# A first block that shares its engines with attention: router columns moved to another bank, loads and steps put in another order

## The chip, the cores and the metric

One core of one Trainium2 chip runs the kernel. The metric is the device time of one execution in microseconds. The median of three runs of the kernel before is 877.84 us (876.73 to 879.01). The engines go by these names: PE is TensorE (PEld its weight loads), DVE is VectorE, ACT is ScalarE, POOL is GpSimd, SP is SyncE, which here issues the DMA transfers in the order in which they are written.

## The reference

Three stages follow each other. The inputs of the attention are 32-bit floats; the weights of the first network come as 64-bit floats.

```python
# attention with a decaying state; B, H, S, D = 4, 8, 768, 48
for t in range(S):
    state = alpha[:, :, t, :, None] * state + einsum('bhd,bhe->bhde', k[:, :, t], v[:, :, t])
    y[:, :, t] = einsum('bhd,bhde->bhe', q[:, :, t], state)
x = y.transpose(0, 2, 1, 3).reshape(3072, 384)
# first network: w_in 384 x 2048, w_out 2048 x 384
h = x @ w_in
x = (h - tanh(h)) @ w_out
# second network: 8 experts, one for each token, w1[e] 384 x 1024, w2[e] 1024 x 384
logits = x @ w_gate;  e = argmax(logits);  p = softmax(logits)[e]
out = p * sigmoid((x @ w_output_gate)[e]) * (relu(x @ w1[e]) @ w2[e])
```

## The kernel before

The 3072 tokens are handled in eight blocks of 384 (`NBLK`, `TB`). For each block, attention has four units (`NP`, a pair of heads each), so unit `u` belongs to block `u // 4`. A unit is worked off in chunks of 64 tokens: `prep_k` (lines 169 to 176) makes the decayed keys `kh`, `prep_q1` and `prep_q2` the products of decays, their reciprocals and the scaled queries `X0`, `scale_k` the keys `kt` divided by the decays, `turn_k` the transposed keys `ktok`. `score` and `causal` give the masked scores, `carry`, `update` and `chain` the states, `readout` the outputs in two PSUM banks (`pair`), and `place` splits them into a rounded part and a rest and stores both with four or six DMAs into `xT`, the input of the first network (lines 307 to 324).

The first network has sixteen steps `f` for each block. `h_step` (lines 402 to 416) multiplies `xT` by the weights' columns (nine matmuls of 384 columns: high times high, high times low, low times high, for three parts of the inner dimension), takes the tanh on ACT, subtracts on DVE, rounds the high half of `gg` on ACT and takes the low half on DVE. `x_step` (lines 418 to 426) multiplies `gg` of the step before by the second weights into three accumulators `px[j][0]` to `px[j][2]`, one PSUM bank each, with nine matmuls of 400 columns: 384 of the output and 16 router columns, which are the second weights already multiplied by `w_gate` and `w_output_gate`.

The weights `WH` and `WL` stay on chip for all blocks; they are made while block 0 runs. For each step `load_w` brings 768 KB of 64-bit floats; `conv` narrows them with three integer instructions on DVE (`narrow`, lines 332 to 337) and issues the load for three steps later; `split_w` rounds the high part on ACT and takes the rest on POOL. `gate_turn` transposes the second weights on PE into the one bank `at` of `psa` and copies them to `wT`; `gate` multiplies `wT` by the router weights into 16 spare columns of an accumulator's bank and copies the high part on ACT; `gate_low` takes the rest on DVE.

Attention of unit 4 to 8 runs within the sixteen steps of block 0, in four phases `ph = f % 4`: scores and states in 0, the mask in 1, the readout in 2, turning and scaling keys in 3. In this block (`first_block`, lines 757 to 807, with the prologue above it) the order of PE, ACT, DVE, POOL and SP is the written one. From block 1 on a planner orders all engines but SP, and from block 2 on SP too. Before block 0 a prologue handles units 0 to 3. `bank` hands out the accumulators' banks in the prologue, and then the bank `at`. A tile's new contents wait until the last reader of the old contents in the same buffer has ended; a PSUM bank is watched as a whole.

Of the kernel before, what the change touches and what calls it, by code (L numbers as in the profile page):

```python
# [63 lines left out]
def tile_kernel(ctx, tc, aps, outs):  # L64
# [16 lines left out]
    ap2 = att.enter_context(tc.tile_pool(name="ap2", bufs=2, side="right"))  # L81
    rw = att.enter_context(tc.tile_pool(name="rw", bufs=2, side="right"))
    stg = att.enter_context(tc.tile_pool(name="stg", bufs=STG, side="right"))
    stg3 = att.enter_context(tc.tile_pool(name="stg3", bufs=2, side="right"))
    psx = mlp.enter_context(tc.tile_pool(name="psx", bufs=1, space=PSUM))
    psh = mlp.enter_context(tc.tile_pool(name="psh", bufs=2, space=PSUM))
    pss = ExitStack()
# [81 lines left out]
    def prep_k(u):  # L169
        s = st[u]  # L170
        a = s["raw"][:, 2 * TB:2 * TB + AW]
        Ex = ap1.tile([128, AW], F32, tag="Ex", name="Ex")
        s["kh"] = ap2.tile([128, NC, CH], F32, tag="kh", name="kh")
        yield dve.tensor_tensor_scan(out=Ex[:, ::-1], data0=a[:, ::-1], data1=ones1[:, ::-1],
                                     initial=0.0, op0=ALU.mult, op1=ALU.add)
        yield dve.tensor_tensor(out=s["kh"], in0=c3(s["raw"][:, 0:TB]), in1=c3(Ex[:, 1:AW])[:, :, 1:CH + 1], op=ALU.mult)
# [40 lines left out]

    def turn_k(u):
        s = st[u]
        ps = bank("pst")  # L220
        for i in range(NA):
            pe.transpose(ps[:, i * 128:(i + 1) * 128], s["kh"].rearrange("p c t -> p (c t)")[:, i * 128:(i + 1) * 128], ident)  # L222
        s["ktok"] = ap1.tile([128, NA, 128], F32, tag="ktok", name="ktok")
        act.copy(s["ktok"].rearrange("p a d -> p (a d)"), ps[:, 0:NA * 128])
# [140 lines left out]
    def gate_turn(f):  # L365
        ps = psa.tile([128, 512], F32, tag="at", name="pso")
        w = gw.pop(f)
        for k in range(KC):
            pe.transpose(ps[:, k * 128:(k + 1) * 128], w[:, DM + k * 128:DM + (k + 1) * 128], ident)
        gated[f] = wT = g3.tile([128, KC, 128], F32, tag="gg", name="wT")  # L370
        act.copy(wT.rearrange("p k c -> p (k c)"), ps[:, 0:DM])

    def gate(f):

        wT = gated.pop(f)
        pl = px[0][f % NA][:, DG + f // NA * 2 * E:DG + (f // NA + 1) * 2 * E]
        for k in range(KC):
            pe.matmul(pl, wT[:, k], wg[:, k], start=(f < 2 and k == 0), stop=(k == KC - 1), skip_group_check=True)
        c = slice(2 * DM, 2 * DM + 2 * E)
        act.copy(WH[:, f, c], pl)  # L380
        gated[f] = pl, c

    def gate_low(f):
        pl, c = gated.pop(f)
        dve.tensor_tensor(out=WL[:, f, c], in0=pl, in1=WH[:, f, c].bitcast(F32), op=ALU.subtract)  # L385

    def conv_next():
        nonlocal nconv
        nconv += 1
        return conv(nconv - 1)  # L390
# [25 lines left out]
        return gg  # L416

    def x_step(j, f, gg):
        if f == 0 and j:
            px[j] = [psx.tile([128, 512], F32, tag=f"x{a}", name=f"x{a}") for a in range(NA)]  # L420
        for a in range(NA):
            n = 0
            for gi, w in ((0, WH), (1, WH), (0, WL)):
                pe.matmul(px[j][a][:, 0:DG], gg[:, gi, a * 128:(a + 1) * 128], w[:, f, DM:],  # L424
                          start=(f == 0 and n == 0), stop=(f == NF - 1 and n == 2))
                n += 1
# [312 lines left out]
    K(NP)  # L739
    fill(4)  # L740
    weave(*half)
    split_w(1)
    gate_turn(0)
    h_begin(0, 0, range(KC - 1))
    weave(prep_q(NP))
    fill(12)
    h_begin(0, 1, range(KC - 1))
    alpha_low(NP)
    load_w_v(NP)
    load_w_v(NP + 1)  # L750
# [1 line left out]
    load_unit(NP + 2)  # L752
    dve.tensor_copy(trib, cst[:, 192:320])
    dve.tensor_copy(base, cst[:, 368:376])
    px[0] = [psx.tile([128, 512], F32, tag=f"x{a}", name=f"x{a}") for a in range(NA)]

    def first_block(f, pend):
        u, ph = NP + (f + 1) // 4, f % 4
        if ph == 0:
            carry(u)  # L760
        elif ph == 1:
            weave(causal(u))
        elif ph == 2:
            weave(prep_k(u + 1))
        else:
            weave(prep_q1(u))
        new = [conv_next()] if nconv < NF else []

        def head():

            gate(f)
            if ph == 0:
                score(u)
                update(u)
                load_v(u + 2)
            elif ph == 2:
                readout(u)
                load_unit(u + 3)
                load_w_v(u + 2)
            elif ph == 3:  # L780
                turn_k(u)
            for g in new:
                next(g, 0)
                next(g, 0)

        def middle():
            weave(*new)
            if ph == 0:
                weave(chain(u))
            elif ph == 3:  # L790
                scale_k(u)
                weave(prep_q2(u))

        gg = h_step(0, f, (head, middle))
        gate_low(f)
        if ph == 2:
            place(u)
        if pend:
            x_step(*pend)
        if new:  # L800
            split_w(f + 2)
        if f + 1 < NF:
            gate_turn(f + 1)
        if ph == 3:
            decay(u)
            alpha_low(u)
        return gg

    pend = None
# [381 lines left out]
```

## Time and profile before

| what | value |
|---|---|
| median of three runs | 877.84 us |
| the profiled execution | 873.37 us |
| its span, first to last instruction | 871.2 us |
| PE busy | 817.5 us, 94% |
| PE weight loads busy | 768.2 us, 88% |
| DVE busy | 473.2 us, 54% |
| ACT busy | 353.8 us, 41% |
| POOL busy | 160.9 us, 18% |

The prologue reaches to about 42 us, block 0 from there to 167, blocks 1 to 7 to 620, and the experts come after. Busy times are of one execution; idle time of an engine that nothing waits for costs nothing. In rows of a timeline the last column in brackets is the idle time ahead of the instruction and what ended it.

### The profile page before, as it was taken

How to read it: one execution, taken by the hardware profiler on the slowest of the kernel's cores; microseconds unless marked ns; L12 is line 12 of the kernel's file. 1: busy time of each engine (PE TensorE's matmuls, PEld its weight loads, DVE VectorE, ACT ScalarE, POOL GpSimd, SP SyncE). 2: the span in 40 equal slices, each digit the busy share in tenths (PEclk: the TensorE clock that was granted, in tenths of full speed). 3: DMA queues.
4: the chain of work that ended last, by engine and by line, in shares of the span. 5: the costliest groups of instructions: out<-in, count | busy, mean ns of one | idle time of the engine just before them, and what ended most of it. 6: DMA issues, size and time to landing. Idle time of an engine off the chain costs nothing.

```text
span 871.2 us, 16990 instructions
## 1 busy us (share of the span) xinstructions
PE 817.5 (94%) x6736; PEld 768.2 (88%) x6736; DVE 473.2 (54%) x1002; ACT 353.8 (41%) x767; POOL 160.9 (18%) x136
## 2 busy tenths in 40 slices
PE   6787867899999999999999999999999999999995
PEld 4576757799999999999899999999999999999995
DVE  7785876656655556565565563355543433434421
ACT  5444533533444434344343343235443434435431
POOL 0122312002010010010020020011233234324321
PEclk9778987999999999999999999999999999999998
DMA  9545343375323223223232320104264154245400
GB/s 273 172 155 164 105 132 90 120 239 167 97 84 98 68 82 97 65 87 93 67 89 65 94 63 22 28 29 145 95 218 154 65 188 169 87 154 199 150 25 28
DMA packets 64358, 98.54 MB, mean 113 GB/s; under 512 B 20235, under 2 KB 52768, under 8 KB 64272
## 3 DMA queue, kind: packets, MB, share of 16 engines
q1 hardware_dynamic: 60864, 87.91, 32.7%
q0 software_dynamic: 3408, 9.47, 2.9%
q8 instruction: 55, 0.90, 0.4%
q14 instruction: 31, 0.25, 0.1%
HBM read 72.13 MB, written 16.25 MB: 101 GB/s over the span
## 4 chain that ended last, share of the span: by engine, by line
PE 72%; issue 5%; DMA 3%; DVE 2%; ACT 1%; SPq 1%; POOL 1%; POOLq 0%; DVEq 0%; ACTq 0%
PE x L424 22%; PE psh L400 20%; PE o L949 10%; PE psf L921 10%; PE psy L302 3%; PE psy L238 2%; PE psu L264 2%; PE pst L900 1%; DMA wst<-wio 1%; PE pst L222 1%; DMA xT<-y 1%; DMA s<-w 1%; POOL out L967 1%; DMA raw<-raw 1%; SPq L321 0%
## 5 line engine op out<-in xcount | busy, mean ns | idle before, releaser
L424 PE MATMUL x<-WH,gg 128*128 128x400 f32 x768 | 219.8, 363 | 26.2 <-DVE WL L385 25.9
L400 PE MATMUL psh<-xT,WH 128*128 128x384 f32 x768 | 207.9, 348 | 2.7 <-DMA xT<-y 2.3
L424 PEld LDWEIGHTS x<-WH,gg 128*128 128x128 f32 x768 | 138.3, 192 | 36.3 <-DVE WL L385 30.1
L400 PEld LDWEIGHTS psh<-xT,WH 128*128 128x128 f32 x768 | 142.6, 194 | 3.8 <-issue 1.7
L410 DVE TENSOR_TENSOR t<-psh,t 128x384 f32<-128x384 f32 x128 | 71.1, 556 | 127.0 <-ACT t L406 118.0
L424 PE MATMUL x<-WL,gg 128*128 128x400 f32 x384 | 134.4, 350 | 0.0
L400 PE MATMUL psh<-xT,WL 128*128 128x384 f32 x384 | 132.4, 345 | 0.0
L406 ACT ACTIVATE t<-psh 128x384 f32<-128x384 f32 x128 | 62.9, 492 | 164.8 <-PE psh L400 162.4
L949 PE MATMUL o<-hi,hh 128*128 128x384 f32 (+2 forms) x440 | 115.1, 338 | 0.0
L921 PE MATMUL psf<-xe,hi 128*128 128x256 f32 (+6 forms) x432 | 109.4, 338 | 0.0
L412 ACT CAST gg<-t 128x384 fp32r<-128x384 f32 x128 | 65.9, 515 | 78.9 <-DVE t L410 75.3
L927 DVE SCALAR_TENSOR_TENSOR hh<-psf,hh 128x384 fp32r<-128x384 f32 (+3 forms) x96 | 40.9, 447 | 91.7 <-ACT hh L925 90.7
L415 DVE TENSOR_TENSOR gg<-t,gg 128x384 fp32r<-128x384 f32 x128 | 70.5, 551 | 33.2 <-ACT gg L412 31.6
L949 PEld LDWEIGHTS o<-hi,hh 128*128 128x128 f32 (+2 forms) x440 | 78.2, 184 | 1.2 <-DVE hh L927 0.2
L921 PEld LDWEIGHTS psf<-xe,hi 128*128 128x128 f32 x432 | 75.8, 188 | 2.7 <-issue 0.3
L949 PE MATMUL o<-lo,hh 128*128 128x384 f32 (+1 forms) x232 | 77.7, 337 | 0.0
L400 PEld LDWEIGHTS psh<-xT,WL 128*128 128x128 f32 x384 | 74.2, 193 | 0.0
L424 PEld LDWEIGHTS x<-WL,gg 128*128 128x128 f32 x384 | 73.9, 193 | 0.1
L925 ACT ACTIVATE hh<-psf 128x256 fp32r<-128x256 f32 (+6 forms) x72 | 34.9, 485 | 94.6 <-PE psf L921 77.1
L921 PE MATMUL psf<-xe,lo 128*128 128x256 f32 (+6 forms) x216 | 71.9, 333 | 0.0
L197 POOL TENSOR_TENSOR kt<-kh,rP 128x384 f32<-128x384 f32 x24 | 19.9, 830 | 278.5 <-PE psy L239 152.9
L856 POOL TENSOR_TENSOR lo<-s,hi 128x768 fp32r<-128x768 f32 (+1 forms) x24 | 48.9, 2038 | 94.8 <-ACT hi L855 94.3
(140 smaller groups left out, 1127.6 us busy)
## 6 DMA issues: line engine op xcount, KB each, us to landing
raw<-raw SPq DMA_DIRECT2D x32, 579.5 KB
wst<-wio SPq DMA_DIRECT2D x16, 768.0 KB
s<-w SPq DMA_DIRECT2D x24, 512.0 KB
s<-w SPq DMA_DIRECT2D x32, 384.0 KB
xT<-y SPq DMA_DIRECT2D x96, 72.0 KB
rows<-blank SPq DMA_DIRECT2D x8, 772.0 KB
WV<-vw SPq DMA_DIRECT2D x32, 144.0 KB
VZ<-vn SPq DMA_DIRECT2D x60, 72.0 KB
```

The source lines that it names most:

```text
L302: pe.matmul(o, w, m, start=(c + x == 0), stop=(x == 1), skip_group_check=True)
L400: pe.matmul(begun[f][:, 0:TB], w[:, f, c], xT[j][:, x, kc], start=(kc + n == 0), stop=(kc == KC - 1 and n == 2))
L406: act.activation(out=t, in_=ps[:, 0:TB], func=AF.Tanh)
L410: dve.tensor_tensor(out=g, in0=ps[:, 0:TB], in1=t, op=ALU.subtract)
L412: act.copy(gg[:, 0], g)
L415: dve.tensor_tensor(out=gg[:, 1], in0=g, in1=gg[:, 0].bitcast(F32), op=ALU.subtract)
L424: pe.matmul(px[j][a][:, 0:DG], gg[:, gi, a * 128:(a + 1) * 128], w[:, f, DM:], start=(f == 0 and n == 0), stop=(f == NF - 1 and n == 2))
L856: (dve, pool)[i % 2].tensor_tensor(out=lo, in0=t, in1=hi.bitcast(F32), op=ALU.subtract)
L921: pe.matmul(ps[:, 0:n], w[:, kc, fs], xe[:, x, kc], start=(i == 0), stop=(i == 3 * KC - 1))
L925: act.activation(out=hh[:, 0:n], in_=ps[:, 0:n], func=AF.Relu)
L927: dve.scalar_tensor_tensor(out=hh[:, o:o + c.stop - c.start], in0=ps[:, c], scalar=0.0, in1=hh[:, c].bitcast(F32), op0=ALU.max, op1=ALU.su ...
L949: pe.matmul(po[q][m][0:p.stop - p.start, 0:DM], hh[:, p], w[:, f], start=(f == 0 and i == 0), stop=(f == NFE - 1 and i == len(parts) - 1))
```

## The change

- The router columns no longer lie in an accumulator's bank but in columns 384 to 400 of the bank in which the second weights were just transposed. ACT copies them once unrounded to `gl` in SBUF and once rounded to `WH`; `gate_low` reads `gl`. The accumulators of block 0 are taken at the first `x_step`.
- In each step of block 0 the next step's weights are split first and the weights of the step after that narrowed first, all three instructions on end; before, narrowing stood around the tanh and its subtraction, and the split at the step's end. The narrowed weights get a third buffer, the keys `kh` one buffer instead of two.
- `x_step` moves from behind `gate_low` to between the rounding of `gg`'s high half and the taking of its low half. `causal` and `prep_k` of phase 1, `prep_k`'s place (phase 2 before) and `prep_q1` of phase 3 move behind it; `decay`, `alpha_low` and `carry` move to the heads of phases 0, 1 and 0.
- `load_unit` moves from the head of phase 2 (for unit `u + 3`) to the end of the next phase 1, behind `alpha_low`; `load_w_v` moves behind `place`.
- Later units' keys are turned in the readout's pair of banks.
- In the prologue the second weight split and the first six matmuls of step 1 go; step 0 and step 1 have them.

```diff
-    stg3 = att.enter_context(tc.tile_pool(name="stg3", bufs=2, side="right"))
+    stg3 = att.enter_context(tc.tile_pool(name="stg3", bufs=3, side="right"))
...
-        s["kh"] = ap2.tile([128, NC, CH], F32, tag="kh", name="kh")
+        s["kh"] = ap1.tile([128, NC, CH], F32, tag="kh", name="kh")
...
-        ps = bank("pst")
+        ps = bank("pst") if u <= NP else pair("pst")[:, 0]
...
-        gated[f] = wT = g3.tile([128, KC, 128], F32, tag="gg", name="wT")
+        wT = g3.tile([128, KC, 128], F32, tag="gg", name="wT")
         act.copy(wT.rearrange("p k c -> p (k c)"), ps[:, 0:DM])
+        gated[f] = wT, ps[:, DM:DG]
 
     def gate(f):
-
-        wT = gated.pop(f)
-        pl = px[0][f % NA][:, DG + f // NA * 2 * E:DG + (f // NA + 1) * 2 * E]
+        wT, pl = gated.pop(f)
         for k in range(KC):
-            pe.matmul(pl, wT[:, k], wg[:, k], start=(f < 2 and k == 0), stop=(k == KC - 1), skip_group_check=True)
+            pe.matmul(pl, wT[:, k], wg[:, k], start=(k == 0), stop=(k == KC - 1), skip_group_check=True)
         c = slice(2 * DM, 2 * DM + 2 * E)
+        gl = ap2.tile([128, 2 * E], F32, tag="gl", name="gl")
+        act.copy(gl, pl)
         act.copy(WH[:, f, c], pl)
-        gated[f] = pl, c
+        gated[f] = gl, c
 
     def gate_low(f):
-        pl, c = gated.pop(f)
-        dve.tensor_tensor(out=WL[:, f, c], in0=pl, in1=WH[:, f, c].bitcast(F32), op=ALU.subtract)
+        gl, c = gated.pop(f)
+        dve.tensor_tensor(out=WL[:, f, c], in0=gl, in1=WH[:, f, c].bitcast(F32), op=ALU.subtract)
...
-        if f == 0 and j:
+        if f == 0:
...
-    split_w(1)
     gate_turn(0)
     h_begin(0, 0, range(KC - 1))
     weave(prep_q(NP))
     fill(12)
-    h_begin(0, 1, range(KC - 1))
...
     def first_block(f, pend):
         u, ph = NP + (f + 1) // 4, f % 4
-        if ph == 0:
-            carry(u)
-        elif ph == 1:
-            weave(causal(u))
-        elif ph == 2:
-            weave(prep_k(u + 1))
-        else:
-            weave(prep_q1(u))
-        new = [conv_next()] if nconv < NF else []
+        if f + 1 < NF:
+            split_w(f + 1)
+        if nconv < NF:
+            weave(conv_next())
 
         def head():
 
             gate(f)
             if ph == 0:
+                if f:
+                    decay(u)
+                carry(u)
                 score(u)
                 update(u)
-                load_v(u + 2)
+            elif ph == 1:
+                if u > NP:
+                    alpha_low(u)
             elif ph == 2:
                 readout(u)
-                load_unit(u + 3)
-                load_w_v(u + 2)
-            elif ph == 3:
-                turn_k(u)
-            for g in new:
-                next(g, 0)
-                next(g, 0)
 
         def middle():
-            weave(*new)
+            if pend and ph != 3:
+                x_step(*pend)
             if ph == 0:
                 weave(chain(u))
+            elif ph == 1:
+                weave(causal(u))
+                weave(prep_k(u + 1))
             elif ph == 3:
+                x_step(*pend)
+                turn_k(u)
+                weave(prep_q1(u))
                 scale_k(u)
                 weave(prep_q2(u))
 
         gg = h_step(0, f, (head, middle))
         gate_low(f)
-        if ph == 2:
+        if ph == 0:
+            load_v(u + 2)
+        elif ph == 1:
+            if u > NP:
+                load_unit(u + 2)
+        elif ph == 2:
             place(u)
-        if pend:
-            x_step(*pend)
-        if new:
-            split_w(f + 2)
+            load_w_v(u + 2)
         if f + 1 < NF:
             gate_turn(f + 1)
-        if ph == 3:
+        else:
             decay(u)
             alpha_low(u)
+            load_unit(u + 2)
         return gg
```

## Rows read from the trace of the kernel before

**Rows 1.** Busy time by stretches: length, busy of each engine (instructions), clock, DMA, GB/s.

```profile
41.80:167.40 125.60, 98.76 (x823) 91.67 (x823) 86.23 (x133) 52.20 (x127) 30.72 (x18) 0.86 0.39 124
71.80:100.80 29.00, 21.94 (x197) 20.39 (x196) 21.38 (x33) 13.53 (x33) 7.47 (x4) 0.96 0.47 150
186.00:252.00 66.00, 66.00 (x638) 62.01 (x636) 40.52 (x92) 26.85 (x63) 10.37 (x13) 1.00 0.49 146
```

**Rows 2.** Waits from 41 to 158 us: us in total, times, longest.

```profile
PE x L424 <- DVE WL L385: 25.9, 14, 5.8
...
DVE w L332 <- DMA wst<-wio: 14.5, 4, 5.2
```

**Rows 3.** Timeline of SP's queue from 50 to 76 us: start, duration, instruction.

```profile
51.50 0.34 SPq L345 DMA_DIRECT2D wst<-wio  x1
74.04 0.33 SPq L151 DMA_DIRECT2D raw<-raw  x1
...
74.90 0.42 SPq L345 DMA_DIRECT2D wst<-wio  x1
```

**Rows 4.** Timeline of DVE, the narrowing of the weights loaded at 74.90.

```profile
82.51 0.56 DVE L332 TENSOR_SCALAR w<-wst 128x768 int32<-128x768 int32 x1 [3.92 <-DMA wst<-wio]
```

**Rows 5.** Timeline of POOL and DVE: a split, instructions beside splits, one without.

```profile
86.35 2.12 POOL L362 TENSOR_TENSOR WL<-w,WH 128x768 fp32r<-128x768 f32 x1 [6.62 <-ACT WH L361]
86.87 2.02 DVE L176 TENSOR_TENSOR kh<-raw,Ex 128x384 f32<-128x384 f32 x1
...
93.61 1.64 DVE L187 TENSOR_SCALAR rP<-P 128x6 f32<-128x6 f32 x1
...
6.62 0.56 DVE L176 TENSOR_TENSOR kh<-raw,Ex 128x384 f32<-128x384 f32 x1
```

**Rows 6.** The tile of loaded weights: the second narrowing instruction, ns minimum, median, maximum.

```profile
L334 DVE SCALAR_TENSOR_TENSOR w<-wst,w x16: 957/959/960, 23.4 to 145.4; 128x768 int32<-128x768 int32 x16
```

**Rows 7.** Timeline of ACT and PE from 97 to 105 us.

```profile
97.86 1.55 ACT L200 ACTIVATE kt<-kh,rP 128x64 f32<-128x64 f32 x6
...
101.14 0.48 ACT L371 COPY wT<-pso 128x384 f32<-128x384 f32 x1 [1.01 <-PE pso L369]
...
102.49 0.74 PE L378 MATMUL x<-wg,wT 128*128 128x16 f32 x6
...
104.65 0.64 PE L424 MATMUL x<-WH,gg 128*128 128x400 f32 x2
```

**Rows 8.** Timeline of PE, the first matmuls behind a stand.

```profile
68.12 1.03 PE L424 MATMUL x<-WH,gg 128*128 128x400 f32 x2 [3.41 <-DVE WL L385]
```

**Rows 9.** Timeline of DVE and ACT in the prologue: keys made and scaled, units 1 to 3.

```profile
13.83 1.54 ACT L200 ACTIVATE kt<-kh,rP 128x64 f32<-128x64 f32 x6
...
14.31 0.56 DVE L176 TENSOR_TENSOR kh<-raw,Ex 128x384 f32<-128x384 f32 x1
...
19.28 0.56 DVE L176 TENSOR_TENSOR kh<-raw,Ex 128x384 f32<-128x384 f32 x1
...
19.62 1.54 ACT L200 ACTIVATE kt<-kh,rP 128x64 f32<-128x64 f32 x6
```

**Rows 10.** Timeline of PE and DVE in block 1 and 2: turning keys and the place.

```profile
214.14 0.49 PE L222 MATMUL pst<-cst,kh 128*128 128x128 f32 x3
214.59 0.56 DVE L311 TENSOR_TENSOR y<-psy,y 128x384 fp32r<-128x384 f32 x1
...
262.76 0.53 DVE L311 TENSOR_TENSOR y<-psy,y 128x384 fp32r<-128x384 f32 x1
...
264.14 0.49 PE L222 MATMUL pst<-cst,kh 128*128 128x128 f32 x3
```

**Rows 11.** Timeline of ACT: first eviction of an accumulator behind blocks 0, 1 and 2.

```profile
166.34 0.48 ACT L462 COPY r<-x 128x384 f32<-128x384 f32 x1 [0.87 <-PE x L424]
...
236.84 0.47 ACT L462 COPY r<-x 128x384 f32<-128x384 f32 x1
...
303.12 0.47 ACT L462 COPY r<-x 128x384 f32<-128x384 f32 x1
```

More of the change, by code (lines that the diff above doesn't have):

```diff
@@ L754, in tile_kernel @@
     dve.tensor_copy(base, cst[:, 368:376])
-    px[0] = [psx.tile([128, 512], F32, tag=f"x{a}", name=f"x{a}") for a in range(NA)]
     def first_block(f, pend):
         u, ph = NP + (f + 1) // 4, f % 4
-        if ph == 0:
-            carry(u)
-        elif ph == 1:
-            weave(causal(u))
-        elif ph == 2:
-            weave(prep_k(u + 1))
-        else:
-            weave(prep_q1(u))
-        new = [conv_next()] if nconv < NF else []
+        if f + 1 < NF:
+            split_w(f + 1)
+        if nconv < NF:
+            weave(conv_next())
         def head():
```

## The prediction

> **What bounds the kernel now.** I read the busy time by stretches first. In the steady part PE is busy for 66.00 of 66.00 us at full clock; in the first block, 125.6 us long, it is busy for 98.8, with the clock at 0.86 [rows 1]. So the first block holds what can be won, and everything behind it moves with its end. Then the waits of that stretch: PE stands 25.9 us, 14 times, in `x_step` for `gate_low`'s write to `WL`, and VectorE stands 14.5 us, 4 times, for a weight load [rows 2]. The first wait is an order, not work: the router columns lie in an accumulator's bank, so the previous step's `x_step` waits until `gate_low`, the last of this step's VectorE work on it, has read them. The second comes from SP's queue: behind 51.50 nothing is issued until 74.04, where the load of a raw unit leads, the values' load follows, and the weight load is third, at 74.90 [rows 3]. The narrowing of those weights starts at 82.51, after 3.92 us of standing [rows 4].
>
> **The parts.** *Router columns.* ScalarE gets one more copy of 16 columns in each step: above nothing, and below the 0.48 of the 384-column copy [rows 7], 16 x 0.48 = 7.7 us at most; I take half of it. ScalarE is busy for 13.53 of 29.0 us in four steps [rows 1], so it is hidden; without that cover it costs the 4. The 25.9 us of `x_step`'s waits go. What is late next is VectorE's own queue.
>
> *VectorE's sum.* It is busy for 21.38 us in the second group of four steps [rows 1]. In it two instructions were held while GpSimd ran a `split_w`: the multiply `kh` took 2.02 instead of 0.56, and an instruction of six columns 1.64 [rows 5], some 1.46 each. 21.38 - 2.9 = 18.5; with 33 hand-overs of about 0.02 (an estimate from starts and ends in rows 5) 19.2. The change adds nothing to it, since `gate_low` is one instruction as before. To this come holds. `split_w` now stands one ScalarE copy behind the step's start, just where VectorE narrows, and GpSimd is busy for 7.47 in four steps [rows 1], some 1.83 a split. Whether the narrowing's second and third instruction can be held in this way no row shows: in 16 runs of the second the times are 957, 959 and 960, so none lay beside a split [rows 6]. Bounds for four steps: 0 if they are never held, 7.5 if each split holds VectorE in full. Laying the four steps out, each engine taking its instructions in the written order, two splits fall on VectorE's SBUF work in full, one for 0.7, and one beside an instruction that reads PSUM and a wait: 1.83 + 1.83 + 0.7 = 4.4. I take it, since `kh`, with two SBUF operands as they have, is held.
>
> The Trainium skill says (SBUF — State Buffer, section "SBUF: two separate sides") that the port pair that VectorE shares with GpSimd is an exclusive lock, taken by a VectorE instruction with two SBUF inputs against a GpSimd one that reads SBUF. The hold of `kh`, 2.02 beside 0.56, agrees. By that rule the narrowing's two instructions are held as well, and four steps have the 4.4; if it did not reach them, they would have the 0.
>
> *The turn from phase 3 to phase 0.* In phase 3 ScalarE scales the keys (1.55, six pieces) once VectorE has the reciprocals, and only behind it copies the next step's `wT` (0.48); only then can PE run gate, scores and update, 104.65 - 102.49 = 2.16 at full clock [rows 7], and then VectorE its chain. 1.45 + 0.48 + 2.16 and four hand-overs of 0.05 are 4.3. VectorE has beside it X0, the low half of gg, the router's low half, a narrowing and a subtraction: 0.5 + 0.5 + 0.1 + 2.5 + 0.5 = 4.1. At full clock it stands for 0.2; but PE has then stood for some 4 us itself, and behind a stand of 3.41 us two matmuls took 1.03 that take 0.64 at full clock [rows 7, 8]. I double PE's 2.16, and VectorE stands for 2.3. With 0.7 for the high half of gg in phase 2 that is 3.0. Four steps: 19.2 + 4.4 + 3.0 = 26.6.
>
> *Unit loads one phase later.* `load_unit` now waits for the `alpha_low` of its own step and no longer stands on SP through two steps ahead of a weight load. Weights then have three steps, 3 x 6.6 = 20 us, against the 7.6 from 74.90 to 82.51 [rows 3, 4]. The 14.5 us go. On SP the values' load still waits for the `update` of its step and the stores for `place`, each within its step, so nothing else is late. If loads stay late, they cost the 14.5.
>
> *Sixteen steps.* First four: 26.6 less PE's stand ahead of the first gate (4.1 as laid out), less six of step 0's nine matmuls, done earlier (1.0), less a first `decay` (0.9): 20.6. Two groups of 26.6. The last has the closing `x_step` with its wait, 1.9, on top: 28.5. Sum 102.3. The old order laid out in the same way gives 109 against 125.6 measured, 16.6 short, of which the late weights are 14.5; for the other 2.1 and for clock I add 3. That makes 105.3, 20.3 less than now.
>
> *Keys in one buffer.* This costs. In the prologue `kh` of unit 2 is written at 14.31 while unit 1's is being scaled, until 13.83 + 1.54 = 15.37: 1.1 late. The scaling of unit 2 moves along from 19.62 to 20.72 and ends at 22.26, and `kh` of unit 3, due at 19.28 + 1.1, waits 1.9 [rows 9]. 3.0 in all; everything up to the first block stands behind it on VectorE. Bounds 1.0 (if slack in the stores' queue takes up two) to 3.3; I take 3.0.
>
> *Third buffer for narrowed weights, second split, six matmuls of step 1.* The first lets a narrowing start without waiting for the transposes; that is in the sum. The split now stands on ScalarE behind the scaling, in PE's wait for the first stores. The matmuls (1.0) lay in that wait and now stand in step 1, under VectorE's work; bare they cost the 1.0.
>
> *Keys turned in the readout's banks.* PE now waits there for `place`. Once in the steady part `place` ends at 214.59 + 0.56 = 215.15, while the turn started at 214.14; in another unit it ends at 263.29 and the turn starts at 264.14, 0.85 later [rows 10]. Bounds for each of 23 later units: 0 to 1.0; I take 0, the second, which has a whole block of settled steps before it.
>
> *Into the next block.* From the first eviction to the second there are 70.50 us, from the second to the third 66.28 [rows 11]: 4.2 are lost at the start of block 1, where the last stores stand behind a unit load. Bounds 0 to 4.2; I take 2.
>
> **Sum.** -20.3 + 3.0 - 2.0 = -19.3 on the profiled 873.37 (span 871.2 and 2.17 around it): 854.1. That execution lies 4.47 under the median of 877.84, so on the scale of the runs 858.5.
>
> **Rivals.** *The narrowing isn't held.* Three groups lose 4.4 and, with PE ready sooner at full clock, some 1.0 of standing each: 858.5 - 3 x 5.4 = 842. For it: none of 16 was seen held; against it: `kh`. Chance 0.15.
>
> *The waits come back elsewhere.* PE stands at the gate behind ScalarE, at half clock, in more steps than the one in four laid out: a group is 29 again as now [rows 1], and only the late weights of the other groups are won. 3 x 2.4 less, and 4 of the first and last: 870. For it: laid out, the new order is only 7 under the old. Against it: the late weights are measured. Chance 0.18.
>
> *Turning keys in the readout's banks costs the steady part, where PE has no slack.* Place: the turn behind `place` in blocks 1 to 7. Price: 23 x 1.0 [rows 10] = 23 us; it decides from 19.3 / 23 = 0.84 us a unit. 858.5 + 23 = 881.5, slower. For it: 66.00 of 66.00 busy, and 215.15 against 214.14. Against it: the 0.85 in hand once steps have settled. Chance 0.07.
>
> *It doesn't do what it says.* Another tie between the accumulators and the end of VectorE's step keeps `x_step`'s wait; the late weights go, but a narrowing at the head of the queue with its hold takes that back, and the prologue's 3 stay: 879. Chance 0.05.
>
> **Numbers.** My forecast has 0.55, with its own range of 850 to 866. A measurement of this kernel can tell some 0.3%, 2.6 us, from no change. Faster: 0.55 + 0.15 + 0.15 of the third case = 0.85; same: 0.05; slower: 0.07 + 0.03 = 0.10. The range takes in the unheld narrowing and the returned waits: 840 to 874.
>
> **What would show it.** `x_step` no longer waits for `WL`, and the waits for weight loads are gone. PE's one long stand in four steps is at the gate's matmuls, for `wT`. Narrowing instructions of 2 to 3 us stand beside splits; always 0.96 would mean 842. Groups take 26 to 27 us, and the first step starts near 45 instead of 41.8. A steady part with PE under 66 of 66, or a first block over 115 us, would make the prediction wrong.

## The result, and the profile after

The changed kernel takes 844.96 us (median of 4 runs, 844.46 to 846.36); beside it the kernel before took 877.29 (4 runs, 874.32 to 879.01). The ratio is 0.9637, with a 95% interval of 0.9608 to 0.9667. The forecast was 858.5, with its own range 850 to 866 and the wide one 840 to 874: faster, as said, but by 32.3 us where 19.3 were forecast, so 844.96 lies outside the first range and inside the second. The profiled execution took 845.42 us, its span 843.6.

Busy time by stretches, of the changed kernel (length, busy of each engine, clock, DMA, GB/s): the first block, one group of four steps in it, and one settled interval. They answer to [rows 1].

```profile
45.26:150.12 104.86, 92.76 (x813) 88.38 (x813) 84.64 (x134) 51.90 (x147) 30.19 (x18) 0.90 0.46 149
70.58:96.50 25.92, 22.69 (x195) 21.72 (x195) 21.78 (x34) 13.18 (x38) 8.13 (x4) 0.90 0.52 166
213.56:279.06 65.50, 65.50 (x644) 62.06 (x643) 40.70 (x90) 26.82 (x65) 6.98 (x7) 1.00 0.30 83
```

The first block takes 104.86 us; 105.3 were forecast. A settled interval takes 65.50 where it was 66.28 [rows 11], and PE is busy for all of it in both.

Waits from 41 to 158 us, of the changed kernel (us in total, times, longest); they answer to [rows 2].

```profile
PE pso L377 <- ACT wT L371: 10.5, 4, 3.6
DVE t L411 <- ACT t L407: 10.5, 5, 4.6
...
DVE SS L268 <- PE psu L264: 7.6, 4, 2.3
```

`x_step` no longer waits for `WL`, and no wait of VectorE for a weight load is left. What is there instead is what was forecast: PE at the gate, for `wT`, and VectorE at its chain, at most 2.3 us at a time. Not forecast is the middle line, VectorE's wait for the tanh: 4.58 us ahead of the first step's subtraction, and 0.89 and 1.51 in the two settled groups of four steps.

The tile of loaded weights (ns minimum, median, maximum), and a timeline of POOL and VectorE at one of its splits. They answer to [rows 6] and [rows 5].

```profile
L334 DVE SCALAR_TENSOR_TENSOR w<-wst,w x16: 957/960/2534, 27.1 to 128.9; 128x768 int32<-128x768 int32 x16
L336 DVE SCALAR_TENSOR_TENSOR w<-wst,w x16: 957/958/2540, 28.1 to 129.9; 128x768 int32<-128x768 int32 x16
```

```profile
62.87 2.12 POOL L362 TENSOR_TENSOR WL<-w,WH 128x768 fp32r<-128x768 f32 x1 [5.16 <-DVE y L311]
...
63.33 2.48 DVE L334 SCALAR_TENSOR_TENSOR w<-wst,w 128x768 int32<-128x768 int32 x1
...
65.85 0.96 DVE L336 SCALAR_TENSOR_TENSOR w<-wst,w 128x768 int32<-128x768 int32 x1
```

The narrowing that started inside the split ends 0.8 us behind it and takes 2.48; the next one, behind the split, 0.96.

Timeline of ACT and PE at the turn from phase 3 to phase 0; it answers to [rows 7].

```profile
94.55 1.54 ACT L200 ACTIVATE kt<-kh,rP 128x64 f32<-128x64 f32 x6 [0.42 <-DVE rP L188]
95.99 0.46 ACT L371 COPY wT<-pso 128x384 f32<-128x384 f32 x1
...
96.50 1.46 PE L377 MATMUL pso<-wg,wT 128*128 128x16 f32 x6 [3.23 <-ACT wT L371]
```

PE stood 3.23 us for the copy behind the scaling, and then ran at half clock (granted 0.50 from 96.50 to 100): six gate matmuls in 1.46 instead of 0.74.

The start of the first step, the last keys of the prologue, and the first eviction behind each of three blocks, of the changed kernel; they answer to [rows 9] and [rows 11].

```profile
23.00 0.56 DVE L176 TENSOR_TENSOR kh<-raw,Ex 128x384 f32<-128x384 f32 x1 [2.00 <-ACT kt L200]
...
45.26 0.58 PE L401 MATMUL psh<-xT,WH 128*128 128x384 f32 x2 [1.22 <-DMA xT<-y]
...
150.12 0.84 ACT L463 COPY r<-x 128x384 f32<-128x384 f32 x2
...
213.56 0.48 ACT L463 COPY r<-x 128x384 f32<-128x384 f32 x1
...
279.06 0.48 ACT L463 COPY r<-x 128x384 f32<-128x384 f32 x1
```

In the two profiled executions the first eviction comes 16.22 us earlier, the second another 7.06 (63.44 after the first instead of 70.50), and each settled interval gives 0.78 more.

### The profile page after: what moved, and what is told of

The parts are those of the page before. It is cut to its first block, busy times and chain, and to the rows that moved or that the text cites. A ratio compares the mean times of both kernels' runs of the same rounds, so it can differ in the third digit from the quotient of the medians.

```text
span 843.6 us, 17092 instructions
## 1 busy us (share of the span) xinstructions
PE 806.4 (96%) x6736; PEld 761.5 (90%) x6736; DVE 478.1 (57%) x1002; ACT 350.5 (42%) x783; POOL 164.0 (19%) x136
## 4 chain that ended last, share of the span: by engine, by line
PE 80%; DVE 6%; issue 5%; DMA 3%; ACT 2%; SPq 1%; POOL 1%; POOLq 0%; DVEq 0%; ACTq 0%
PE x L425 24%; PE psh L401 22%; PE o L950 11%; PE psf L922 10%; PE psy L302 4%; PE psy L238 3%; PE psu L264 2%; DVE w L334 2%; DMA raw<-raw 2%; PE pst L222 1%; PE pst L901 1%; ACT kt L200 1%; PE pso L377 1%; DMA s<-w 1%; DVE w L336 1%
## 5 line engine op out<-in xcount | busy, mean ns | idle before, releaser
L425 PE MATMUL x<-WH,gg 128*128 128x400 f32 x768 | 215.4, 356 | 1.0 <-DVE gg L416 0.7
L401 PE MATMUL psh<-xT,WH 128*128 128x384 f32 x768 | 204.2, 343 | 1.3 <-DMA xT<-y 1.2
L425 PEld LDWEIGHTS x<-WH,gg 128*128 128x128 f32 x768 | 140.5, 191 | 6.2 <-DVE gg L416 1.7
L401 PEld LDWEIGHTS psh<-xT,WH 128*128 128x128 f32 x768 | 138.4, 189 | 3.1 <-issue 1.6
L401 PE MATMUL psh<-xT,WL 128*128 128x384 f32 x384 | 130.1, 339 | 0.0
L416 DVE TENSOR_TENSOR gg<-t,gg 128x384 fp32r<-128x384 f32 x128 | 73.7, 575 | 52.6 <-ACT gg L413 51.9
L197 POOL TENSOR_TENSOR kt<-kh,rP 128x384 f32<-128x384 f32 x24 | 20.3, 845 | 273.0 <-PE psy L239 230.8
L401 PEld LDWEIGHTS psh<-xT,WL 128*128 128x128 f32 x384 | 72.4, 189 | 0.6
```

The source lines that it names most:

```text
L401: pe.matmul(begun[f][:, 0:TB], w[:, f, c], xT[j][:, x, kc], start=(kc + n == 0), stop=(kc == KC - 1 and n == 2))
L416: dve.tensor_tensor(out=gg[:, 1], in0=g, in1=gg[:, 0].bitcast(F32), op=ALU.subtract)
```

## The experiments

The table has every kernel that ran; gate, block and intervals are from one profiled execution of each. The medians of the kernel before, which ran beside each set, were 876.7 to 879.6. "Gate" is the start of the first gate's matmuls, "block" the time from there to the first eviction, and "2nd" and "3rd" the intervals between evictions. Most expectations count the first block from some 41.8 us (45.26 in the changed kernel), so their figures lie 0.6 to 2.4 us above these. The gate itself comes 2.4 us apart in e5 and e9, which have the same prologue; a difference of that size in it says nothing.

| kernel | median us | ratio, 95% | gate | block | 2nd | 3rd |
|---|---|---|---|---|---|---|
| before (profiled 873.37) | 877.3 | 1 | 43.46 | 122.88 | 70.50 | 66.28 |
| before again (879.14) | one run | | 43.73 | 123.70 | 74.60 | 66.28 |
| changed | 844.96 | 0.9608-0.9667 | 45.86 | 104.26 | 63.44 | 65.50 |
| e1 kh in two buffers | 841.84 | 0.9578-0.9641 | 42.21 | 104.08 | 64.01 | 65.50 |
| e2 keys in the general bank | 849.77 | 0.9663-0.9719 | 45.30 | 102.32 | 65.68 | 66.28 |
| e3 unit loads alone | 866.71 | 0.9842-0.9908 | 43.70 | 121.53 | 66.93 | 66.27 |
| e4 router alone | 860.35 | 0.9783-0.9840 | 44.21 | 110.01 | 70.52 | 66.33 |
| e5 both | 848.29 | 0.9663-0.9727 | 41.77 | 101.27 | 69.78 | 66.33 |
| e6 GpSimd writes zeros | 839.96 | 0.9563-0.9637 | 53.72 | 87.16 | 63.36 | 65.50 |
| e7 turn first | 839.62 | 0.9563-0.9617 | 40.33 | 102.17 | 63.64 | 65.50 |
| e8 x ahead | 839.20 | 0.9555-0.9608 | 41.67 | 101.71 | 63.38 | 65.50 |
| e9 both, and the bank | 841.91 | 0.9561-0.9637 | 44.18 | 100.14 | 64.89 | 65.48 |
| e10 and the turn first | 841.55 | 0.9556-0.9634 | 42.66 | 101.19 | 65.21 | 65.63 |
| e12 and ScalarE's queue | 836.82 | 0.9505-0.9565 | 42.13 | 95.87 | 65.28 | 65.59 |

**e1: keys in two buffers again**

```
-s["kh"] = ap1.tile([128, NC, CH], F32, tag="kh", name="kh")
+s["kh"] = gp.tile([128, NC, CH], F32, tag="t", name="kh") if u in (1, 3) else ap1.tile([128, NC, CH], F32, tag="kh", name="kh")
```

> The changed kernel, with the products kh of units 1 and 3 in another buffer, so that the prologue again alternates between two. If the one buffer is what made the prologue late (the first step of the first block starts at 45.26 instead of 41.79), that step starts near 41.8 again, nothing else moves, and the time falls by 3.0 to 3.5 us from 844.96, to some 841.7. Rival: the buffer isn't what is late, the moved split of weights or the stores are: the start stays at 45 and the time at 845.

841.84, 3.1 us less, and nothing behind the prologue moved by more than 0.6: the same block, the same settled intervals. In the changed kernel the keys of the prologue waited three times for the scaling before, 0.74, 0.76 and, at 23.00, 2.00 us; here the last ones come without a wait:

```profile
18.60 0.56 DVE L176 TENSOR_TENSOR kh<-raw,Ex 128x384 f32<-128x384 f32 x1
```

So the one buffer is what made the prologue late, and not the moved split or the stores.

**e2: keys in the general bank again**

```
-ps = bank("pst") if u <= NP else pair("pst")[:, 0]
+ps = bank("pst")
```

> The changed kernel, with the keys of all units turned in the general bank again, as before. Theory A: the choice of bank made the steady blocks 65.50 us long instead of 66.28, because it changes the order in which PE takes its groups of matmuls; then blocks are near 66.3 again, PE busy throughout, and six or seven of them give 4.7 to 5.5 us: some 850. Theory B: the shorter steady blocks come from another part of the change (one buffer for kh); blocks stay at 65.5 and the time at 845. Theory C, a rival of the prediction: the turn in the readout's banks costs something there; then it gets faster than 845.

849.77, 4.8 us more, and the settled interval is 66.28 again: theory A. What differs is the order of PE's groups of matmuls. First the readout of one unit before, in the general bank's order, then in the changed kernel (timeline of PE).

```profile
240.89 0.46 PE L302 MATMUL psy<-X,SS 48*64 48x64 f32 x6
241.28 0.81 PE L424 MATMUL x<-WH,gg 128*128 128x400 f32 x3
...
242.82 0.34 PE L424 MATMUL x<-WL,gg 128*128 128x400 f32 x1
...
243.10 0.34 PE L302 MATMUL psy<-X,WV 64*64 64x64 f32 x6
...
244.08 0.28 PE L302 MATMUL psy<-X,WV 64*64 64x64 f32 x2
```

```profile
221.73 0.47 PE L302 MATMUL psy<-X,SS 48*64 48x64 f32 x8
222.01 0.30 PE L302 MATMUL psy<-X,WV 64*64 64x64 f32 x8
222.13 0.42 PE L302 MATMUL psy<-X,SS 48*64 48x64 f32 x8
222.37 0.30 PE L302 MATMUL psy<-X,WV 64*64 64x64 f32 x8
222.48 0.42 PE L302 MATMUL psy<-X,SS 48*64 48x64 f32 x8
222.72 0.30 PE L302 MATMUL psy<-X,WV 64*64 64x64 f32 x8
```

Before, the planner lets six matmuls of a readout go ahead, puts `x_step` between, and the rest follows; of the four readouts of a block one is cut so. Taken from the start of each piece to the start of the group behind it, the readouts of a block take 5.23 us in five pieces before, 5.24 in this kernel, and 4.86 in four pieces after. The scores, too, are in five pieces before and in four after (3.52 and 3.38 us). PE doesn't change from group to group less often: from the same point of one block to that of the next there are 59 groups before and in this kernel, and 60 after. `h_step` takes 0.34 us less in as many pieces and `x_step` 0.06 more in three more; with the readouts' 0.37 and the scores' 0.14 that is the 0.78, to a hundredth. So the bank changes the planner's order, and with PE busy throughout the order is time; what one change of group costs isn't shown. In the first block this kernel was 1.9 us shorter, and its second interval 2.2 longer: the two together are 168.00 against 167.70.

**e3 and e4: unit loads alone, router columns alone**

```
     elif ph == 2:
         readout(u)
-        load_unit(u + 3)
...
         alpha_low(u)
+        load_unit(u + 2)
```

> The kernel before, with nothing changed but the place of the unit loads in the first block: each behind its own step's alpha_low, one phase later. If the forecast's term is right, VectorE's 14.5 us of waits for weights go, the first block takes some 111 us instead of 125.6, and the start of the next one gains up to 2: 861 to 863 against 877.3. Rival: the late weights lay beside PE's waits for the router columns and were partly hidden by them; those waits grow and the gain is under 8: over 869.

866.71: 10.8 us less in the medians, between the forecast and the rival, but of that only 1.35 in the first block of the profile (868.48, near the slow end of six executions from 862.63 on). VectorE's wait for loads is gone, and it waits longer for the tanh and for a buffer. The first view is of this kernel; the second is of the kernel before, which had 7.7 us of the wait for a buffer already:

```profile
DVE t L410 <- ACT t L406: 14.1, 11, 4.4
...
DVE w L332 <- issue: 11.8, 5, 4.2
```

```profile
DVE w L332 <- issue: 7.7, 3, 4.2
```

One of these stands (timeline of VectorE):

```profile
72.60 0.56 DVE L332 TENSOR_SCALAR w<-wst 128x768 int32<-128x768 int32 x1 [4.16 <-issue]
```

The view names no releaser for it. The narrowing at 72.60 had its weights; by the program it stands until PE has turned the weights that lie in its output buffer, one of two, and PE turns them (at 71.66) only behind `x_step`, which waits for `WL` (20.3 us in all, 25.9 before). So the rival was right for the first block: the late weights lay under the router's tie. The other gain is at the next block's start: its interval is 66.93 instead of 70.50, or instead of 74.60 by the second profile of the kernel before (e11).

```
-pl = px[0][f % NA][:, DG + f // NA * 2 * E:DG + (f // NA + 1) * 2 * E]
+wT, pl = gated.pop(f)          # pl: columns DM:DG of the bank of the turned weights
...
+act.copy(gl, pl)
```

> The kernel before, with nothing changed but the router columns: out of the accumulators' banks and into the bank of the turned weights (the carry is issued behind the gate's matmuls, as it has to be). The late weights stay. If the 25.9 us of x_step's waits are a tie of their own, most of them come back at VectorE, which is behind by the late weights: a first block of 117 to 121 us, 869 to 873. Rival: with the tie gone PE stands as long elsewhere, at the gate's matmuls or at the next step's: a first block over 124, no gain, 876 or more. Other rival: the two terms are independent, the waits go in full and only the late weights are left: a first block under 112, under 865.

860.35, a first block of 110.01 (112.4 as the expectation counts), 12.9 less than before: more than the first theory gives, and near the third. `x_step`'s wait is gone; of it 12.3 us come back at the gate, and the late weights stay:

```profile
PE pso L378 <- ACT wT L371: 12.3, 6, 4.0
...
DVE w L332 <- DMA wst<-wio: 11.2, 3, 4.0
```

**e5: both, and nothing else**

e4's edit and e3's in one kernel.

> The kernel before with two parts of the change and no more: the router columns out of the accumulators' banks, and the unit loads one phase later. Alone the first part left a first block of 112.4 us (from 124.5) in which VectorE still waited 11.2 us for weights; the second alone left one of 123.4. Theory A: the two waits covered each other, and with the router's tie gone the late weights cost in full; both together give a first block of 101 to 105 us and 842 to 848 us in all, and what else the change does in the first block (narrowing first, three buffers, split earlier) brings next to nothing. Theory B: the gains only add (12.1 and 1.1): a first block of some 111 us, 852 to 856. Theory C: without the third buffer VectorE waits at the narrowing for the transposes instead of the weights: 106 to 110 us, and the third buffer is what brings the rest.

A first block of 101.27: 21.6 less than before, where the two alone gave 12.9 and 1.35. They don't add: once the tie is gone the late weights are bare and cost 8.7 (110.01 to 101.27). Theory A. The block is even 3.0 shorter than the changed kernel's: the rest of the change costs there, on balance, and which part of it does, no run shows. The second and third narrowing instructions are never held here, as the tile of loaded weights shows for the second:

```profile
L334 DVE SCALAR_TENSOR_TENSOR w<-wst,w x16: 957/959/961, 22.1 to 123.7; 128x768 int32<-128x768 int32 x16
```

GpSimd's splits hold other instructions instead: VectorE is busy for 88.48 us in this block, and for 84.64 in the changed kernel's. So held narrowing alone doesn't explain the 3.0.

What this kernel lacks comes later: a second interval of 69.78 (PE busy for 68.05 of it) and settled ones of 66.3. Why the moved loads don't shorten the second interval here, as they did in e3, wasn't found out.

**e6: GpSimd writes zeros**

```
-pool.tensor_tensor(out=WL[:, f, c], in0=gw[f], in1=WH[:, f, c].bitcast(F32), op=ALU.subtract)
+pool.memset(WL[:, f, c].bitcast(F32), 0.0)
```

> The changed kernel, with GpSimd writing zeros into the low halves of the first layer's weights instead of subtracting (the low halves are left out), so that it reads nothing beside VectorE's narrowing. The second and third narrowing instructions should take 0.95 us in all runs, where some take 2.5. If the holds are worth what the prediction gave them (4.4 us a group, and PE's standing with them), groups fall from 26 to 21 or 22 us: 13 to 16 us less, 829 to 832. Rival: VectorE has waits of its own in a group (for the tanh and for the states' sums) that take the freed time: groups of 24 or more, under 6 us gained, over 839.

839.96 in all looks like the rival; the profile shows why it isn't. The zeros depend on nothing, so GpSimd wrote all of them at the start, and a VectorE instruction of the prologue stood through it (below); the first gate comes 7.86 us late, at 53.72. From there on the block takes 87.16 instead of 104.26, and its groups 20.2, 21.3 and 21.3 instead of 24.7, 25.9 and 26.7: 4.6, 4.6 and 5.4 less each; 5.4 were forecast for the holds and PE's standing together. This profiled execution, 836.05, is the fastest of four; by the medians, and if the gate is as late in all four, the gain behind it is 5.0 and 7.86, 12.9 us, where 13 to 16 were expected in the total. In the changed kernel's first block no wait of another engine is put down to GpSimd, so the holds are the only cost of the split that the trace shows. The same group and the same tile as shown above of the changed kernel:

```profile
73.90:95.20 21.30, 20.45 (x196) 19.57 (x196) 18.83 (x34) 13.18 (x38) 0.00 (x0) 1.00 0.61 202
```

```profile
L334 DVE SCALAR_TENSOR_TENSOR w<-wst,w x16: 957/959/960, 34.0 to 121.3; 128x768 int32<-128x768 int32 x16
```

VectorE's busy time falls from 21.78 to 18.83 in the group, and PE has the full clock, 1.00 instead of 0.90. So the holds themselves are 2.95 of the 4.6 us; the rest are VectorE's own stands, 3.76 in the changed kernel's group and 2.09 here.

**e7 and e8: the turn first, and x ahead**

```
     weave(prep_q1(u))
+    if f + 1 < NF:
+        gate_turn(f + 1)      # in phase 3; no longer at the step's end there
     scale_k(u)
```

> The changed kernel with kh in two buffers (worth 3.1 us alone) and, in phase 3, the next step's weights turned and copied by ScalarE ahead of the scaling of the keys. PE's stands at the gate's matmuls for wT (3.2 to 3.6 us, three of them) should go. If they set the turn from phase 3 to phase 0, as forecast (VectorE stands 2.3 us for the sums there), 4 to 7 us come on top: 835 to 838. Rival: the scores need the scaled keys and stand in their place: only what kh gives, 841 to 842.

839.62 with the two buffers, 2.2 less than those alone: between the forecast and the rival. PE's stand at the gate falls from 10.5 us to 4.7, and the next one comes behind it, for the carry's copy on ScalarE:

```profile
PE psu L264 <- ACT psu L255: 4.8, 3, 1.7
PE pso L377 <- ACT wT L371: 4.7, 4, 1.7
```

```
     if ph == 0:
         if f:
             decay(u)
+            x_step(*pend)      # no longer behind the scores and the update
         carry(u)
         score(u)
```

> As the kernel with the turn first, and in phase 0 the accumulating matmuls of the previous step go ahead of the scores, so that PE works (some 2 us) while ScalarE scales the keys. If PE's stand behind the gate is what delays the sums, it is covered and PE's clock holds: 1 to 3 us less than that kernel. Rival: these matmuls wait for the low half of the previous step's gg, which VectorE writes last, and the sums come later: 1 to 3 us more.

839.20: no difference that can be told from e7, so neither the forecast nor the rival. PE has the work, and the carry is covered, but the turn of the weights now waits for the later sums:

```profile
PE pso L369 <- DVE SS L268: 5.0, 4, 1.9
PE x L425 <- DVE gg L416: 1.6, 3, 0.6
```

**e9, e10 and e12: what is needed, and a better kernel**

e9 is e5 with the bank of the changed kernel (e2's line, reversed).

> The kernel before with three parts of the change: router columns out, unit loads one phase later, and the keys turned in the readout's banks from unit 5 on. With the first two alone the first block took 101.3 us, shorter than the changed kernel's 104.9, but the second interval between evictions was 69.78 (63.44 in the changed kernel) and the later ones 66.3 to 66.6. Theory A: the bank sets the order of PE's groups in all later blocks, the second included: 63.5 to 65.7 there, 65.5 after it, and 838 to 841 against 848.3. Theory B: the bank sets only the settled blocks; what is lost in the second interval comes from the first block's own order: 68 to 70 there, 843 to 845. The first block itself stays within 1.5 us of 101.3 by both.

841.91, 0.9 above the range of theory A, and as much as the changed kernel with its keys in two buffers (e1, 841.84). The settled intervals are 65.48, and the second falls from 69.78 to 64.89: theory A, the bank's order decides there, too. So three parts of the change bring as much as all of it does with two buffers; the rest brings nothing in the total, and the one buffer for keys costs 3.1. e10 is e9 with e7's edit.

> As the kernel with three parts, and in phase 3 the next step's weights are turned and copied ahead of the scaling of the keys. In the kernel with two parts PE stood 7.0 us, 4 times, at the gate's matmuls for wT. If those stands can be had here, where no narrowing is held by GpSimd and VectorE has room, the first block loses 3 to 6 us; in the changed kernel the same step brought some 2. Rival: the scores wait for the scaled keys as there: under 2 us. Best of all by the first: 833 to 837.

841.55: no gain, the rival. PE's stand at the gate falls from 8.9 us in e9 to 2.9, but PE's waits name the next one, and ScalarE's timeline what lies ahead of it:

```profile
PE psu L264 <- ACT psu L255: 7.4, 3, 2.5
PE pso L378 <- ACT wT L371: 2.9, 5, 1.0
```

```profile
90.69 0.82 ACT L361 CAST WH<-w 128x768 fp32r<-128x768 f32 x1
91.41 0.70 ACT L192 ACTIVATE GE<-P 128x288 f32<-128x288 f32 x1
...
92.11 0.60 ACT L215 ACTIVATE raw<-raw,amin 128x384 f32<-128x384 f32 x1
...
92.71 0.46 ACT L408 ACTIVATE t<-psh 128x384 f32<-128x384 f32 x1
...
93.33 0.25 ACT L255 COPY psu<-SS 128x48 f32<-128x48 f32 x1
```

The decay (`GE`) and `alpha_low` (`raw`) stand ahead of the tanh and the carry's copy, and nobody needs them so early.

```
     if ph == 0:
         carry(u)
+        if f:
+            decay(u)             # was at the end of phase 3, with the two below
...
+    elif ph == 1:
+        if u > NP:
+            alpha_low(u)
+            load_unit(u + 2)
```

> As the kernel with three parts and the turn first; besides, in ScalarE's queue the activation of decay (0.9 us) goes behind the carry's copy of the next step, and that of alpha_low (0.8), with the unit load behind it, one step later, as in the changed kernel. With the turn first, PE no longer stood at the gate but 2.5 us, three times, for the carry's copy, which lay behind these two and the split's copy on ScalarE. If ScalarE's queue is now what sets the turn from phase 3 to phase 0, some 1.7 us of each of three turns go: 5 us, 835 to 838 against 841.55. Rival: VectorE's instructions between (X0, the halves of gg, a narrowing) take the time instead: under 2 us, 840 or more.

836.82, 4.7 us less, the fastest of all here (0.9535 of the time before, 0.9505 to 0.9565). The first block loses 5.3. Stretches of it, first of e10 and then of this kernel:

```profile
42.66:143.85 101.19, 89.87 (x813) 84.15 (x813) 89.45 (x135) 53.97 (x147) 32.05 (x18) 0.93 0.48 153
```

```profile
42.13:138.00 95.87, 85.94 (x813) 78.40 (x813) 91.61 (x135) 53.37 (x148) 32.00 (x18) 1.00 0.51 162
```

Of the 5.3, PE's stands give only 1.4 (11.32 to 9.93); 3.9 are the same 813 matmuls at a clock of 1.00 instead of 0.93. In e10 the clock fell to half (1.2 of 2.4 GHz) behind stands of up to 2.5 us; here the longest for the carry is 1.2, and it stayed at full. That is the account of two executions, and the gain doesn't hang on the clock alone: two others of this kernel took 836.07 and 836.41 at a mean clock of 0.984 and 0.982, while e10 took 840.16 to 841.10 at 0.983.

VectorE is now busy for 91.61 of 95.87 us; in e6, where no split held it, it was busy for 72.94 in the block. So holds, on other instructions than the narrowing now, are some 18 us of VectorE's time here: an estimate, as e6 has another order.

**e11: the kernel before, once more**

> The kernel before once more, unchanged, for a second profile of it. Its timed runs spread over 8 us (870.9 to 880.0), those of the changed kernel over 2; the profiled execution of 873.37 lies in the lower part. If the spread comes from transfers in the first block (late weights) and at the start of the second, the first evictions of this execution differ from 166.34 and 236.84 by what its time differs from 873.37, and the steady intervals are the same 66.28; if it comes from the clock or the experts' part, the first evictions agree within 0.5 us.

This execution took 879.14, 5.8 us more than the profiled one that the forecast was made from. Its second eviction is 5.2 late, of which 4.1 arise in the second interval (the first interval's end, then the second's, by ACT's timeline):

```profile
167.43 0.48 ACT L462 COPY r<-x 128x384 f32<-128x384 f32 x1 [0.88 <-PE x L424]
...
242.03 0.47 ACT L462 COPY r<-x 128x384 f32<-128x384 f32 x1
```

In it PE is busy for 69.59 of 74.60 us at a clock of 0.95; in the first profile it was 67.91 of 70.50 at 0.98. The next interval is 66.28 in both. So of the difference between these two executions most lies at the start of the second block, and 1.1 in what comes before it; that the whole spread lies there isn't shown by two.

## Why the prediction came out as it did

**Right in the mechanism, and in the sum in part by luck.** The tie of the router columns and the late weights bound the first block; VectorE binds it now. The layout gave four steps 26.6 and the block 105.3: measured are 25.9 and 26.7 for the two settled groups, and 104.86. The holds were the disputed term, 4.4 a group against 0: the narrowing is held (2.48 and 2.54 beside 0.96). The rival without holds, 842, lies close to the measured time, and e6 refutes it all the same. So the rule of the Trainium skill (SBUF — State Buffer, section "SBUF: two separate sides") held here for the narrowing's second and third instructions, which no row of before had shown. A row that the prediction didn't use pointed the same way: before, the first narrowing instruction, with one operand in SBUF, took 1.87 us at 133.10, inside a split that started at 132.33, and 0.56 as a rule.

The parts of the sum were off both ways. The holds are some 3 us a group (VectorE's busy time in the changed kernel less that in e6: 2.95 and 3.16), and not 4.4; VectorE's stands, put at 3.0, are 3.8 and 4.4, since its wait for the tanh was left out. The first four steps were put at 20.6 and took 25.3: PE's stand was taken off a group in which VectorE alone is busy for 22.0. The last group, 26.9 where 28.5 were laid out, and the 3 us added for the clock made up for most of it.

The turn from phase 3 to phase 0 is where it was forecast: three stands at the gate of 3.2 to 3.6 us, and 2.3 at the chain. The one buffer for keys was put at 3.0; the first step came 3.47 late, and e1 gives 3.1.

**Right as a sum, wrong in its parts.** The forecast read the first block's loss as 14.5 us of late weights and a tie, each by itself, and took the shortfall of the old order's layout (16.6) for late weights. e3 shows that alone they were worth 1.35 there, in its profiled execution, since the same narrowing would have waited for its buffer; e5 shows 8.7 once the tie is gone. Two waits on one path cover each other. It did no harm because the new block was laid out from its own instructions, and not got by taking waits off the old one.

**Wrong, three terms.** The forecast had 19.3 less on the profiled execution; measured are 27.95 (873.37 to 845.42).

- *Into the next block*: 2.0 were taken, from bounds of 0 to 4.2; the second interval lost 7.06, from 70.50 to 63.44. The loads alone bring it to 66.93 (e3), the whole change without the bank to 65.68 (e2); but loads and router columns together leave it at 69.78 (e5), so what the loads do there stays open. Of the last 2.24 most is work that moved across the eviction: block and interval together are 168.00 without the bank and 167.70 with it, and PE is busy for 63.28 us in this interval where a settled one has 65.50. The upper bound of 4.2 took a settled interval for the least that was possible.
- *Keys turned in the readout's banks*: taken at 0, with a rival that they cost 23. They gain 0.78 in each settled interval, and 1.88 and 1.12 in the two intervals in which the kernel before had more than that; 4.56 in these four, as e2's four intervals confirm (4.55), of which the next gives back 0.42. A bound below nothing was missing, against a steady part where PE was busy for 66 of 66 us: the bank changed the order of PE's work, and that was not weighed.
- *The scale*: 4.47 us were added because the profiled execution lay under the median. e11, a single execution, lies 5.8 above the first profile, and 4.1 of that sit at the start of the second block, in the very time that the change shortens. The changed kernel's profile is within 0.5 us of its median. So most of these 4.47 should have been gained, not carried over.

Together: 8.65 on the profile (5.06 and 4.15 of the two terms up to the last eviction, 1.1 back from the first block's end, 0.5 behind the last eviction), 4.47 of the scale and 0.5 of the changed kernel's own profile are the 13.5 us by which the forecast was too high. The first block's end was forecast 17.3 earlier, and came 16.22.

**The other rivals.** Waits did come back at the gate, but in one step of four, as laid out, and not in more. Turning keys in the readout's banks costs the steady part nothing. No other tie kept `x_step`.

## What to carry to other kernels

Lay out the new order from its own instructions, and don't add up waits taken off the old one: two waits on one path cover each other, and the second shows its price only when the first is gone. Where an engine is busy all the time, a change of buffer can still change the time, by the order that a planner then finds; give such an edit a bound on both sides. Compare the parts of a layout with the profile, too, and not only its sum: here they were off both ways. And take a second profile of the kernel before, or look at how far its runs spread: where the spread sits in the stretch that is changed, it can belong to the gain.

## What the runs showed of the hardware that wasn't expected

In e6 GpSimd's 16 writes of zeros, which read nothing, held one VectorE instruction of six columns for 6.50 us (0.17 in the changed kernel), while two others beside them, each with two operands in SBUF, took what they take elsewhere (0.56 and 0.97). Timeline of POOL and VectorE:

```profile
2.81 10.93 POOL L362 MEMSET WL<- 128x768 f32 x16
```

```profile
5.80 0.56 DVE L176 TENSOR_TENSOR kh<-raw,Ex 128x384 f32<-128x384 f32 x1
6.28 0.97 DVE L184 TENSOR_TENSOR_SCAN P<-raw,ones 128x391 f32<-128x391 f32 x1
7.28 6.50 DVE L187 TENSOR_SCALAR rP<-P 128x6 f32<-128x6 f32 x1
```

The held one ends as the last write does, at 13.7: it didn't get in between two of the writes. The Trainium skill (SBUF — State Buffer, section "SBUF: two separate sides") tells two kinds apart: an instruction with two SBUF inputs meets only a GpSimd instruction that reads SBUF, while one in a two-port mode of VectorE meets any. For the first kind these rows agree: `kh` is held beside a split [rows 5] and not beside the zeros. For the second they agree if the held instruction ran in such a mode, which no row shows.
